# Both halves of a fold and all five chunks of a gather issued together, in a fused attention and feed-forward kernel

## The chip, the cores and the metric

The kernel runs on one core of a Trainium2 chip. The metric is device time in microseconds (us) of one execution. TensorE is called PE here (its matmuls; PEld is its weight loads), VectorE DVE, ScalarE ACT, GpSimd POOL and SyncE SP, as in the profile. Batches are counted from 0, so that the third batch is batch 2.

## The reference

Attention against 32 memory slots for each of 8 batches and 8 heads, then a feed-forward layer with the gate h cos(h) over all 4608 tokens:

```python
# q, k, v: (8, 8, 576, 64); phi: (8, 8, 576, 32); all float32
a = softmax(phi, axis=memory)                 # weights of each token over the 32 slots
k_m = einsum('bhsm,bhsd->bhmd', a, k)
v_m = einsum('bhsm,bhsd->bhmd', a, v)
attn = softmax(q @ k_m.T / 8) @ v_m           # (8, 8, 576, 64)
x = attn.transpose(0, 2, 1, 3).reshape(4608, 512)
h = x @ w_in                                  # w_in: 512 x 2048
out = (h * cos(h)) @ w_out                    # w_out: 2048 x 512
```

## The kernel before

**The main stream.** The 4608 tokens are worked in 12 groups of 384. For every group there are 16 steps f, one for each 128 of the 2048 hidden columns; a step has a number i = 16 * group + f. In a step `gemm1` (line 539) multiplies the softmax weights `aT` by a folded weight `vw` into the PSUM tile `hp` (6 matmuls of 384 columns, or 12 of 192 where a group spans two batches), `act` and `act_end` (lines 563 and 578) turn `hp` into `gp` on ACT and DVE by turns, and `gemm2` (line 591), four steps behind, multiplies `gp` by `w_out` into three accumulators `acc` (9 matmuls of 512 columns). `hp` has three PSUM buffers (line 80).

**The fold.** Since x = weights * v_m, the product v_m * w_in is formed once for each batch and called `vw`. It is made in four quarters q of 512 hidden columns, each in two halves g (`fold`, line 499). A half is `fold_psum` (line 472): for batches 2 to 7 eight matmuls with weights of 128 rows by 32 columns, four that run side by side in the four column strips of the array with the high part `vp` of the weights, and then four with the low part `vl`. The result is a PSUM tile `pv`, which `split_half` (line 487) reads twice: ACT writes its high part (line 490), then DVE its rest (line 492).

**The preparation of a batch.** `prep(b)` (line 525) is a generator that is advanced in the loop a few pieces at each step. Its first part `memory(b)` (line 273) makes the softmax of `phi`, then gathers k and v into the slots: five chunks of up to 128 tokens, each eight matmuls of 32 weight columns by 129 columns in float32 (line 241; the trace records each of them twice), all into one PSUM tile `psA`. After the last chunk it starts the loads of the next batch's `phi`, k and v, then divides by the sum (`X`, lines 307 to 313), transposes (`tpx`, line 317) and writes k_m and v_m out. Its second part `attend(b)` (line 440) has the scores `sc` (line 386, weights of 64 columns, in three blocks), softmax on DVE and ACT, and the transposes back into `aT`.

**What sets the order.** The tiles `psA`, `tpx`, `sc` and `pv` share one PSUM pool of two buffers, `ps_s` (lines 81 and 83): a third one waits until the first has been read. The first two batches are issued in an order written out by hand (line 50). From there on the loop (line 989) issues the steps; `folds` (line 985) says at which step a half is folded, `jobs` (line 982) between which steps a batch is prepared, and `NSTEP` (line 976) into how many pieces the preparation is counted for spreading it evenly over these steps. A scheduler then moves the issued instructions on each engine by their dependences.

Of the kernel before, what the change touches and what calls it, by code (L numbers as in the profile page):

```python
# [72 lines left out]
def attention_then_ffn(ctx: ExitStack, tc: tile.TileContext, phi, phiT, kv, kv_first, qT, w_in, w_out, eye, out):  # L73
# [9 lines left out]
    def small_ps(name):  # L83
        return ps_s.tile([P, 512], F32, tag="ps_s", name=name)
# [25 lines left out]
    def load_phi(b):  # L110
        if b < NT:
            loads["phiT", b] = t = ld.tile([P, 2, S], F32, tag="phiT", name=f"phiT_{b}", bufs=1)
            nc.sync.dma_start(out=t, in_=phiT[b, :, 0:S].rearrange("(g p) s -> p g s", p=P))
        a = ld.tile([P, 5, HM], F32, tag="phi", name=f"phi_{b}")
        nc.sync.dma_start(out=a[:, 0:4], in_=phi[b, 0:512].rearrange("(c p) m -> p c m", p=P))
        nc.sync.dma_start(out=a[0:S - 512, 4], in_=phi[b, 512:S])
        loads["phi", b] = a

    def load_kv(b):
        ts = []  # L120
        for c, (s0, n) in enumerate(TCH):
            t = ld.tile([P, H * KV], F32, tag="kv", name=f"kv_{b}_{c}", bufs=5)
            nc.sync.dma_start(out=t[:n], in_=kv[b, s0:s0 + n])
            ts.append(t)
        loads["kv", b] = ts
# [110 lines left out]
    def gather(psA, a, kvs, c, wide):  # L236
        n = TCH[c][1]
        for g in range(2):
            for j in range(4):
                h = 4 * g + j  # L240
                nc.tensor.matmul(psA[32 * j:32 * (j + 1), g * KV:g * KV + wide],  # L241
                                 lhsT=a[:n, c, h * M:(h + 1) * M], rhs=kvs[c][:n, h * wide:(h + 1) * wide],
                                 start=(c == 0 and g == 0), stop=(c == 4), skip_group_check=True)

    def blank(b):
        st["km", b] = wk.tile([P, NP, 2 * M], F32, tag="km", name=f"km_{b}", bufs=1)
        st["vm", b] = wk.tile([P, NP, 2 * M], F32, tag="vm", name=f"vm_{b}")
        nc.gpsimd.memset(st["km", b], 0.0)
        nc.gpsimd.memset(st["vm", b], 0.0)

    def spread_k(b, tpx):
        tv = tpx[:, 0:HM].rearrange("p (c t m) -> p c t m", t=2, m=M)
        nc.scalar.mul(st["km", b][0:D, :, 0:M], tv[0:D, :, 0], 1.0 / math.sqrt(D))
        nc.scalar.mul(st["km", b][D:P, :, M:2 * M], tv[D:P, :, 1], 1.0 / math.sqrt(D))
# [4 lines left out]
    def spread_v(b, tpx, copy):  # L259
        tv = tpx[:, 0:HM].rearrange("p (c t m) -> p c t m", t=2, m=M)  # L260
        copy(out=st["vm", b][D:P, :, 0:M], in_=tv[D:P, :, 0])
        copy(out=st["vm", b][0:D, :, M:2 * M], in_=tv[0:D, :, 1])

    def bound(b, X):
        l1 = wk.tile([P, 4], F32, tag="l1", name=f"l1_{b}")
        nc.vector.tensor_reduce(out=l1, in_=X.rearrange("p g (t d) -> p (g t) d", t=2), op=ALU.add, axis=AX.X,
                                apply_absolute_value=True)
        nc.vector.tensor_tensor(out=l1, in0=l1, in1=vmask.rearrange("p g t -> p (g t)"), op=ALU.mult)
        l2 = wk.tile([P, 1], F32, tag="l2", name=f"l2_{b}")
        nc.vector.tensor_reduce(out=l2, in_=l1, op=ALU.max, axis=AX.X)  # L270
        return l2

    def memory(b):
        a = loads.pop(("phi", b))
        if b < NT:

            nmx = wk.tile([P, 2], F32, tag="nmx", name=f"nmx_{b}", bufs=1)
            nc.vector.tensor_reduce(out=nmx, in_=loads.pop(("phiT", b)), op=ALU.max, axis=AX.X)
            top = small_ps(f"top_{b}")[:, 0:HM]
            for g in range(2):  # L280
                nc.tensor.transpose(top[:, g * P:(g + 1) * P], nmx[:, g:g + 1].broadcast_to([P, P]), ident)
        else:
            top = st["top", b]
        yield
        if b >= NT:
            yield
            yield
        for c0, c1, n in ((0, 4, P), (4, 5, S - 512)):
            ins = nc.vector.tensor_tensor(out=a[:n, c0:c1], in0=a[:n, c0:c1],
                                          in1=top[:n].unsqueeze(1).broadcast_to([n, c1 - c0, HM]),  # L290
                                          op=ALU.subtract)
            if b >= NT:

                tc.keep_in_program_order(ins)
            nc.scalar.activation(a[:n, c0:c1], a[:n, c0:c1], AF.Exp)
        yield
        yield
        kvs = loads.pop(("kv", b))
        psA = small_ps(f"psA_{b}")
        for c in range(5):  # L300
            gather(psA, a, kvs, c, KV)
            yield
        if b + 1 < B:
            load_phi(b + 1)
            load_kv(b + 1)
        pv = psA[:, 0:2 * KV].rearrange("p (g x) -> p g x", g=2)
        den = wk.tile([P, 2], F32, tag="den", name=f"den_{b}")
        nc.vector.tensor_scalar(out=den, in0=pv[:, :, 2 * D], scalar1=1e-9, scalar2=None, op0=ALU.add)
        nc.vector.reciprocal(out=den, in_=den)
        X = wk.tile([P, 2, P], F32, tag="X", name=f"X_{b}", bufs=1)  # L310
        for g in range(2):
            nc.vector.tensor_scalar(out=X[:, g], in0=pv[:, g, 0:2 * D], scalar1=den[:, g:g + 1], scalar2=None,
                                    op0=ALU.mult)
        yield
        tpx = small_ps(f"tpx_{b}")
        for g in range(2):
            nc.tensor.transpose(tpx[:, g * P:(g + 1) * P], X[:, g], ident)
        blank(b)
        spread_k(b, tpx)
        spread_v(b, tpx, nc.vector.tensor_copy)  # L320
        yield
        l2 = bound(b, X)
        l3 = wk.tile([P, 1], F32, tag="l3", name=f"l3_{b}")
        nc.gpsimd.partition_all_reduce(l3, l2, channels=P, reduce_op=RED.max)  # L324
        st["l3", b] = l3
        v_scale(b)
        yield


    def v_scale(b):  # L330
        ev = wk.tile([P, 1], F32, tag="ev", name=f"ev_{b}", bufs=2)
        power_of_two(ev, st["l3", b])
        st["ev", b] = ev
# [191 lines left out]
    def prep(b):  # L525
        yield from memory(b)
        yield from attend(b)
# [445 lines left out]
            yield  # L973

    REST = (18, 19, 20, 22, 24, 25)
    NSTEP = 24
    jobs, folds = [], {}
    for b in range(1, B):
        use = 48 * (b // 2) + 16 * (b % 2)
        before, length = {1: (3, 0), 2: (5, 13), 3: (6, 16)}.get(b, (6, 17) if b % 2 else (13, 18))  # L980
        if b > 1:
            jobs.append((b, use - before - length, use - before - 1))
        for q in range(NQ):
            for g in range(2):
                folds.setdefault(use - before + 4 * q + 2 * g, []).append((b, q, g))
    gens = {}
    rest = attend_rest()
    pending, begun = [(0, f, st["gp", f]) for f in range(NF - LAG, NF)], []
    for i in range(NF, 12 * NF):
# [29 lines left out]
        for b, s, e in jobs:  # L1019
# [3 lines left out]
            if s <= i <= e:  # L1023
                if b not in gens:
                    gens[b] = [prep(b), 0]
                want = math.ceil((i - s + 1) * NSTEP / (e - s + 1))
                while gens[b][0] is not None and gens[b][1] < want:
# [54 lines left out]
```

## Time and profile before

| what | value |
|---|---|
| median of 3 runs | 700.62 us (700.43 to 701.5) |
| the profiled execution's own time | 700.91 us |
| its span, first to last instruction | 699.1 us |
| PE busy | 691.4 us |
| DVE busy | 525.9 us |
| ACT busy | 503.1 us |
| POOL busy | 36.9 us |
| granted TensorE clock | 1.000 |

The profile is of one execution. The 1.8 us between its span and its own time lie before the first and after the last instruction. A row of the timeline gives the start of a group of like instructions, its length, the engine, the line, output<-inputs, the shape and how many; in brackets stands idle time before it and what ended that. PE overlaps one matmul with the next, so the time that a matmul takes from the others is the distance of two starts and not its own length.

### The profile page before, as it was taken

What the parts mean: (1) busy time and instruction counts of PE and PEld (TensorE: products, weight loads), DVE (VectorE), ACT (ScalarE), POOL (GpSimd) and SP (SyncE); (2) the same over time, 40 slices, a digit from 0 to 9 for tenths busy, and PEclk for the clock granted to TensorE, in tenths of its full rate; (3) what the DMA queues carried; (4) which work ended last, traced back from release to release, by engine and by line L of the source; (5) the groups of instructions that cost most, each with busy time, mean ns of one, the idle gap of its engine ahead of it and who ended that gap; (6) DMA issues with size and microseconds to landing.
All of it is one profiled execution on the core that took longest, in us unless ns stands there. A gap on an engine that the chain in (4) does not pass through costs nothing.

```text
span 699.1 us, 11806 instructions
## 1 busy us (share of the span) xinstructions
PE 691.4 (99%) x4588; PEld 354.8 (51%) x4588; DVE 525.9 (75%) x1118; ACT 503.1 (72%) x942; POOL 36.9 (5%) x50
## 2 busy tenths in 40 slices
PE   8999999999999999999999999999999999999997
PEld 4444445464544445555445445655445444565553
DVE  4887899999979875689657886589766986566552
ACT  3686888996976966868775876769767776665652
POOL 2423100000001000010000000000000000000000
PEclk9999999999999999999999999999999999999999
DMA  9999827109243100321105300142100100100101
GB/s 291 389 317 362 321 68 201 31 11 282 84 133 103 50 1 13 135 76 63 46 1 171 114 0 1 50 169 68 46 0 2 46 0 1 46 1 1 46 1 45
DMA packets 31480, 66.17 MB, mean 95 GB/s; under 512 B 2176, under 2 KB 11456, under 8 KB 31424
## 3 DMA queue, kind: packets, MB, share of 16 engines
q1 hardware_dynamic: 27104, 57.55, 25.5%
q10 hardware_dynamic: 4320, 7.87, 3.0%
q8 instruction: 36, 0.59, 0.4%
q14 instruction: 20, 0.16, 0.1%
HBM read 51.77 MB, written 9.44 MB: 88 GB/s over the span
## 4 chain that ended last, share of the span: by engine, by line
PE 81%; DVE 10%; ACT 4%; DMA 3%; issue 1%; SPq 0%; POOL 0%; DVEq 0%; ACTq 0%
PE acc L604 40%; PE hp L553 21%; PE acc L599 6%; PE pv L483 4%; PE hp L544 3%; PE psA L241 2%; DVE u L574 2%; PE sc L386 2%; DVE gp L586 1%; DMA phi<-in_phi 1%; DMA kv<-in_kv_first 1%; DVE u L583 1%; PE pvf L509 1%; PE pv L477 1%; ACT u L579 1%; ACT gp L585 1%
## 5 line engine op out<-in xcount | busy, mean ns | idle before, releaser
L604 PE MATMUL acc<-wo,gp 128*128 128x512 f16 x1584 | 372.2, 379 | 0.0
L604 PEld LDWEIGHTS <-gp 128*128 128x128 f16 x1584 | 153.4, 98 | 160.4 <-issue 2.1
L553 PE MATMUL hp<-aT,vw 128*128 128x192 f16 (+1 forms) x1440 | 203.5, 284 | 0.9 <-DVE u L583 0.8
L553 PEld LDWEIGHTS <-vw 128*128 128x128 f16 x1440 | 124.9, 98 | 82.1 <-issue 27.7
L579 ACT ACTIVATE u<-u,quarter 128x384 f32<-128x384 f32 x176 | 106.9, 614 | 68.8 <-DVE u L574 68.3
L583 DVE SCALAR_TENSOR_TENSOR u<-hp,u 128x384 f32<-128x384 f32 x176 | 96.5, 553 | 61.5 <-ACT u L579 60.9
L574 DVE SCALAR_TENSOR_TENSOR u<-hp,cu,gp 128x192 f32<-128x192 f32 (+1 forms) x240 | 115.3, 502 | 24.5 <-ACT gp L569 23.0
L569 ACT ACTIVATE gp<-hp,cu 128x192 int32<-128x192 f32 (+1 forms) x240 | 111.5, 491 | 22.5 <-PE hp L553 15.6
L586 DVE TENSOR_TENSOR gp<-u,gp 128x384 f16<-128x384 f32 x176 | 96.2, 551 | 34.5 <-ACT gp L585 33.9
L585 ACT CAST gp<-u 128x384 f16<-128x384 f32 x176 | 88.4, 509 | 43.9 <-DVE u L583 43.4
L599 PE MATMUL acc<-wo,gp 128*128 128x512 f32 x96 | 44.4, 596 | 0.0
L492 DVE SCALAR_TENSOR_TENSOR vw<-pv,vw 128x512 f16<-128x512 f32 x48 | 33.0, 688 | 7.0 <-ACT vw L490 6.5
L490 ACT ACTIVATE vw<-pv 128x512 f16<-128x512 f32 x48 | 28.4, 591 | 8.0 <-PE pv L483 7.5
L620 ACT ACTIVATE ob<-acc,os 128x512 f32<-128x512 f32 x28 | 18.5, 684 | 14.5 <-PE acc L604 11.9
L599 PEld LDWEIGHTS acc<-wo,gp 128*128 128x128 f32 x96 | 17.6, 191 | 17.9 <-issue 16.0
L544 PE MATMUL hp<-aT,vf 128*128 128x384 f32 x64 | 24.0, 499 | 0.0
L241 PE MATMUL psA<-kv,phi 128*32 128x129 f32 (+3 forms) x640 | 23.6, 276 | 0.2
L579 ACT ACT_TABLE_LOAD x18 | 23.1, 1283 | 0.3
L241 PEld LDWEIGHTS psA<-kv,phi 128*32 128x32 f32 (+1 forms) x640 | 16.1, 109 | 12.0 <-issue 6.9
L386 PE MATMUL sc<-q,km 128*64 128x256 f32 (+3 forms) x192 | 20.0, 336 | 0.1
L324 POOL PARTITION_ALL_REDUCE l<-l x6 | 3.0, 508 | 301.3 <-DVE l L270 301.3
L399 ACT ACT_TABLE_LOAD x14 | 18.0, 1283 | 0.3
(159 smaller groups left out, 544.6 us busy)
## 6 DMA issues: line engine op xcount, KB each, us to landing
kv<-in_kv SPq DMA_DIRECT2D x28, 516.0 KB, 5.5
raw_out<-in_w_out SPq DMA_DIRECT2D x8, 1024.0 KB, 8.1
q<-in_qT SPq DMA_DIRECT2D x7, 1152.0 KB, 5.6
out<-ob ACTq DMA_DIRECT2D x30, 256.0 KB, 2.2
raw_in<-in_w_in SPq DMA_DIRECT2D x6, 1024.0 KB, 12.3
phi<-in_phi SPq DMA_DIRECT2D x7, 512.0 KB, 5.2
w_in_sb<-w_in_parts SPq DMA_DIRECT2D x12, 256.0 KB, 5.6
phiT<-in_phiT SPq DMA_DIRECT2D x4, 576.0 KB, 6.9
```

The costliest lines, as they stand in the source:

```text
L241: nc.tensor.matmul(psA[32 * j:32 * (j + 1), g * KV:g * KV + wide], lhsT=a[:n, c, h * M:(h + 1) * M], rhs=kvs[c][:n, h * wide:(h + 1) * wid ...
L386: nc.tensor.matmul(sc[D * p:D * (p + 1), g * n:(g + 1) * n], lhsT=km[:, 2 * g + p], rhs=qt[:, 2 * g + p, t0:t0 + n], start=True, stop=True)
L544: nc.tensor.matmul(hp[:, :GT], lhsT=st["vf", q][:, g, fo * P:(fo + 1) * P], rhs=st["aTf"][:, g], start=(g == 0), stop=(g == 1))
L553: nc.tensor.matmul(hp[:, c0:c0 + n], lhsT=vw[:, wi, g, fo * P:(fo + 1) * P], rhs=aT[:, ai, g, c1:c1 + n], start=(k == 0), stop=(k == 5))
L569: ins = nc.scalar.activation(ni[:, c0:c0 + n], hp[:, c0:c0 + n], AF.Copy, scale=turns, bias=0.25)
L574: nc.vector.scalar_tensor_tensor(out=u[:, c0:c0 + n], in0=hp[:, c0:c0 + n], scalar=turns, in1=ni[:, c0:c0 + n], op0=ALU.mult, op1=ALU.subt ...
L579: nc.scalar.activation(u, u, AF.Sin, scale=TWO_PI_BELOW, bias=quarter)
L583: nc.vector.scalar_tensor_tensor(out=u, in0=hp[:, :GT], scalar=2.0 ** -17, in1=u, op0=ALU.mult, op1=ALU.mult)
L585: nc.scalar.copy(gp[:, 0], u)
L586: nc.vector.tensor_tensor(out=gp[:, 1], in0=u, in1=gp[:, 0], op=ALU.subtract)
L599: nc.tensor.matmul(accs[grp][t], lhsT=gp[:, t * P:(t + 1) * P], rhs=wo[:, f + 1], start=(f == 0), stop=(f == NF - 1))
L604: nc.tensor.matmul(accs[grp][t], lhsT=gp[:, gi, t * P:(t + 1) * P], rhs=parts[:, wi], start=(f == 0 and gi == 0 and wi == 0), stop=(f == N ...
```

## The change

```diff
         psA = small_ps(f"psA_{b}")
         for c in range(5):
             gather(psA, a, kvs, c, KV)
-            yield
+        yield
         if b + 1 < B:
             load_phi(b + 1)
             load_kv(b + 1)
...
-    NSTEP = 24
+    NSTEP = 20
...
-                folds.setdefault(use - before + 4 * q + 2 * g, []).append((b, q, g))
+                folds.setdefault(use - before + 4 * q + (2 * g if b < 2 else 0), []).append((b, q, g))
```

The five chunks of a gather, until now five pieces of the preparation, become one piece; since the generator has four pieces fewer, `NSTEP` goes from 24 to 20. For batches 2 to 7 the second half of a quarter is folded in the same step as the first, where it came two steps later. No instruction of the computation is added or left out; ACT gets two more loads of an activation table (the order has 19 at line 579 and 15 at line 399, from 18 and 14).

The first place is PE at the gather of batch 2. `psA` is the gathered tile, `kv_0` to `kv_4` are the chunks; the number at the end of a name only tells instances apart.

```order
 L241 MATMUL psA_1472<-kv_0_724,phi_721 32x129 x8
 L241 MATMUL psA_1472<-kv_1_726,phi_721 32x129 x8
 L241 MATMUL psA_1472<-kv_2_728,phi_721 32x129 x8
+L241 MATMUL psA_1472<-kv_3_730,phi_721 32x129 x8
+L241 MATMUL psA_1472<-kv_4_732,phi_721 32x129 x8
 L553 LDWEIGHTS vw_0_774
```

The last two chunks stood one step later, between `gemm2` and the next `gemm1`:

```order
 L604 MATMUL acc_2_1005<-wo,gp_13_1371 128x512
-L241 MATMUL psA_1472<-kv_3_730,phi_721 32x129 x8
-L241 MATMUL psA_1472<-kv_4_732,phi_721 32x129 x8
 L553 LDWEIGHTS vw_0_774
-L553 MATMUL hp_2_1570<-aT_678,vw_0_774 128x384
```

They moved up to the other three, so that the gather of this batch is one run of matmuls instead of two.

The second place is PE at quarter 2 of the fold of batch 4 (`pv_2_0` and `pv_2_1` are its halves), before:

```order
L483 LDWEIGHTS vl
L483 MATMUL pv_2_0_3816<-w_in_sb,vl 32x512
L553 LDWEIGHTS vw_3_3020
L553 MATMUL hp_12_3831<-aT_2229,vw_3_3020 128x384
L553 LDWEIGHTS vw_3_3020
```

and now:

```order
L483 LDWEIGHTS vl
L483 MATMUL pv_2_0_3816<-w_in_sb,vl 32x512
L483 LDWEIGHTS vp_3567
L483 MATMUL pv_2_1_3827<-w_in_sb,vp_3567 32x512
L483 LDWEIGHTS vp_3567
L483 MATMUL pv_2_1_3827<-w_in_sb,vp_3567 32x512
```

Where `gemm1` followed the first half, the second half follows it directly; two steps further on nothing stands in its old place.

The third place is DVE at quarter 1 of the fold of batch 2, while batch 3 is prepared (`vw_1<-pv_1_0` reads the first half, `at<-sc_0` the scores), before:

```order
L492 SCALAR_TENSOR_TENSOR vw_1_2118<-pv_1_0_2119,vw_1_2118 128x512
L586 TENSOR_TENSOR gp_15_2102<-u_15_2101,gp_15_2102 128x384
L574 SCALAR_TENSOR_TENSOR u_0_2156<-hp_0_2149,cu_1938,gp_0_2157 128x384
L229 TENSOR_TENSOR mx_2320<-phi_2130 128x512
L230 TENSOR_TENSOR mx_2320<-mx_2320 128x256
L583 SCALAR_TENSOR_TENSOR u_0_2156<-hp_0_2149,u_0_2156 128x384
L261 COPY vm_2177<-tpx_2173 64x4x32
```

and now:

```order
L492 SCALAR_TENSOR_TENSOR vw_1_2158<-pv_1_0_2159,vw_1_2158 128x512
L586 TENSOR_TENSOR gp_15_2142<-u_15_2141,gp_15_2142 128x384
L492 SCALAR_TENSOR_TENSOR vw_1_2158<-pv_1_1_2170,vw_1_2158 128x512
L574 SCALAR_TENSOR_TENSOR u_0_2198<-hp_0_2191,cu_1938,gp_0_2199 128x384
L392 STREAM_TRANSPOSE at_2182<-sc_0_2185 128x512
```

The two reads of the halves come with one instruction between them instead of eleven, and the read of the scores follows them closely.

Counted over the whole PE order from the gather of batch 2 on, a run being tiled matmuls (weights of 32 or 64 columns) with no matmul of 128 weight columns between them:

| runs that hold | before | now |
|---|---|---|
| gather of batch 2 | 2 | 1 |
| folds of batch 2, gather of batch 3 | 11 | 7 |
| folds of batch 3, gather of batch 4 | 10 | 5 |
| folds of batch 4, gather of batch 5 | 10 | 5 |
| folds of batch 5, gather of batch 6 | 10 | 6 |
| folds of batch 6, gather of batch 7 | 10 | 5 |
| folds of batch 7 | 8 | 4 |
| together | 61 | 33 |
| scores alone | 14 | 15 |

Of the 24 quarters 20 are now one run. The other four (quarters 0 of batches 2 and 5, quarters 3 of batches 3 and 5) are split by steps of the main stream. One run before held a half of a fold and a block of scores together; those scores now stand alone.

## The prediction

> **What bounds the kernel now.** I read the page first (busy times and durations), then the busy time by stretch, then the timeline of PE around single folds, gathers and scores, and last the rows in which PE stands idle. The page:
>
> ```profile
> span 699.1 us, 11806 instructions
> PE 691.4 (99%) x4588; PEld 354.8 (51%) x4588; DVE 525.9 (75%) x1118; ACT 503.1 (72%) x942; POOL 36.9 (5%) x50
> ...
> L604 PE MATMUL acc<-wo,gp 128*128 128x512 f16 x1584 | 372.2, 379 | 0.0
> ...
> L492 DVE SCALAR_TENSOR_TENSOR vw<-pv,vw 128x512 f16<-128x512 f32 x48 | 33.0, 688 | 7.0 <-ACT vw L490 6.5
> L490 ACT ACTIVATE vw<-pv 128x512 f16<-128x512 f32 x48 | 28.4, 591 | 8.0 <-PE pv L483 7.5
> ...
> L579 ACT ACT_TABLE_LOAD x18 | 23.1, 1283 | 0.3
> ```
>
> PE is busy for 99% of the span. The next view says whether that holds in the stretches that the change touches: 289 to 323 prepares a batch, 323 to 366 mostly folds.
>
> ```profile
> core 0: us, PE busy (x) PEld busy (x) DVE busy (x) ACT busy (x) POOL busy (x), PEclk, DMA share, GB/s
> ...
> 289.00:323.00 34.00, 33.60 (x309) 20.02 (x307) 28.48 (x74) 27.14 (x54) 2.15 (x4) 1.00 0.39 124
> 323.00:366.00 43.00, 43.00 (x258) 20.01 (x255) 28.93 (x56) 30.96 (x57) 0.00 (x0) 1.00 0.05 19
> ```
>
> PE has no idle time where a batch is folded and 0.4 us of 34 in the preparation, while DVE and ACT are at 67 to 84%. The clock is full. So time can come only out of PE's own work, or go into new waits of PE. The change adds and removes no matmul; what it can save lies between them. One half of a fold, alone between `gemm2` and `gemm1`:
>
> ```profile
> 208.91 1.03 PE L604 MATMUL acc<-wo,gp 128*128 128x512 f16 x4
> ...
> 209.87 0.10 PEld L483 LDWEIGHTS <-vp 128*32 128x32 f16 x4 [0.42 <-issue]
> 209.87 0.40 PE L483 MATMUL pv<-w_in_sb,vp 128*32 128x512 f16 x4
> 209.88 0.10 PEld L483 LDWEIGHTS <-vl 128*32 128x32 f16 x4
> 210.10 0.39 PE L483 MATMUL pv<-w_in_sb,vl 128*32 128x512 f16 x4
> ...
> 210.42 1.15 PE L553 MATMUL hp<-aT,vw 128*128 128x384 f16 x6
> ...
> 210.54 0.60 ACT L490 ACTIVATE vw<-pv 128x512 f16<-128x512 f32 x1 [0.53 <-PE pv L483]
> ...
> 211.40 1.24 PE L604 MATMUL acc<-wo,gp 128*128 128x512 f16 x5
> ...
> 211.61 0.69 DVE L492 SCALAR_TENSOR_TENSOR vw<-pv,vw 128x512 f16<-128x512 f32 x1
> ```
>
> A group's last matmul starts one matmul length before the group's end. The four `acc` matmuls take 1.03 us and one takes 0.379, so they start (1.03 - 0.38) / 3 = 0.22 apart, and the last starts at 208.91 + 1.03 - 0.38 = 209.56. After it the tiled matmuls should start at 209.78; they start at 209.87, 0.09 late. Their two waves of four are 0.23 apart, about the 0.22 of any 512 columns. The next full matmul should start 0.22 after the second wave and starts 0.32 after. From `acc` to `hp` it is 210.42 - 209.56 = 0.86; less the 0.22 that `acc` takes anyway, the half costs 0.64 us, of which two waves are 0.43 or 0.44. **About 0.2 us goes at the two ends of the run**, where PE changes between full and tiled matmuls and shows as busy.
>
> **The price of a change, from runs that are already joined.** One chunk of a gather alone, and a half joined with one chunk:
>
> ```profile
> 364.98 0.59 PE L604 MATMUL acc<-wo,gp 128*128 128x512 f16 x2
> 365.51 0.65 PE L241 MATMUL psA<-kv,phi 128*32 128x129 f32 x16
> 366.09 0.82 PE L604 MATMUL acc<-wo,gp 128*128 128x512 f16 x3
> ```
> ```profile
> 201.16 0.59 PE L604 MATMUL acc<-wo,gp 128*128 128x512 f16 x2
> 201.69 0.40 PE L483 MATMUL pv<-w_in,vp 128*32 128x512 f16 x4
> 201.91 0.39 PE L483 MATMUL pv<-w_in,vl 128*32 128x512 f16 x4
> 202.13 0.61 PE L241 MATMUL psA<-kv,phi 128*32 128x129 f32 x16
> 202.67 1.15 PE L553 MATMUL hp<-aT,vw 128*128 128x384 f16 x6
> ```
>
> In the same way the chunk costs 366.09 - (364.98 + 0.59 - 0.38) - 0.22 = 0.68, and half and chunk together 202.67 - (201.16 + 0.59 - 0.38) - 0.22 = 1.08. Apart they would be 0.64 + 0.68 = 1.32, so the joint saves 0.24. A half joined with a block of scores, whose weights have 64 columns, and such a block alone:
>
> ```profile
> 216.05 0.59 PE L604 MATMUL acc<-wo,gp 128*128 128x512 f16 x2
> 216.58 0.40 PE L483 MATMUL pv<-w_in_sb,vp 128*32 128x512 f16 x4
> ...
> 217.12 1.08 PE L386 MATMUL sc<-q,km 128*64 128x256 f32 x8
> 218.14 1.15 PE L553 MATMUL hp<-aT,vw 128*128 128x384 f16 x6
> ```
> ```profile
> 307.33 0.81 PE L604 MATMUL acc<-wo,gp 128*128 128x512 f16 x3
> 308.07 1.08 PE L386 MATMUL sc<-q,km 128*64 128x256 f32 x8
> 309.09 1.08 PE L553 MATMUL hp<-aT,vw 128*128 128x192 f16 x11
> ```
>
> Together 218.14 - 216.26 - 0.22 = 1.66, the scores alone 309.09 - (307.33 + 0.81 - 0.38) - 0.22 = 1.11: this joint saves only 0.64 + 1.11 - 1.66 = 0.09, since the tile shape still changes inside it.
>
> **The change part by part.**
>
> *The runs.* By the count above the PE order has 61 - 33 = 28 fewer runs of folds and gathers. Twenty are quarters whose halves now touch. No run of before has two halves in a row, so this price is estimated: by its two waves a half costs 0.43 within a run against 0.64 alone, which saves 0.21; the ends are 0.09 (different tile shapes) and 0.24 (half and chunk, same shape). I take 0.21, since the two halves have one shape. 20 x 0.21 = 4.2 us. The other eight are joints with or inside gathers, at 0.24: 1.9 us. The scores that no longer touch a half give back 0.09. On PE together 4.2 + 1.9 - 0.1 = **6.0 us**, all of it where PE sets the pace.
>
> *The second half comes two steps earlier.* ACT and DVE then get the reads of both halves in one step: 2 x 0.59 and 2 x 0.69 us, where they had one each. With the pair such a step lasts longer on PE, by 0.64 + 0.43 us, so about half of these reads is paid by the step itself; the rest delays `gp`, which `gemm2` needs four steps later. At 67 and 72% busy in the folding stretch that is caught up; I take nothing. If that cover is gone, the price is that of the second rival below.
>
> *Two buffers of `ps_s`.* A pair holds both, so whatever needs one next waits for the DVE read of the first half. That read ended at 211.61 + 0.69 = 212.30, 2.43 us after the half had begun. Nearly everywhere the next user comes one preparation piece or four steps later. At quarter 1 of batch 2 and quarter 3 of batch 6 it is a block of scores after only one `gemm1`: counted from the pair's start, the fourth wave starts after 0.23 + 2 x 0.22 = 0.67, the first `hp` matmul 0.32 later, and the scores after six of these (211.40 - 210.42 = 0.98) and the 0.09 of a run's beginning: 2.06 us in all. The scores come 2.43 - 2.06 = 0.4 us too early. Price between nothing (DVE free at once) and 0.4 each; I take 0.2 + 0.2 = 0.4 us.
>
> *Waits that stood before.* PE's idle rows from batch 2 on that are longer than 0.25 us:
>
> ```profile
> 186.58 0.59 PE L604 MATMUL acc<-wo,gp 128*128 128x512 f16 x2
> 187.53 0.65 PE L553 MATMUL hp<-aT,vw 128*128 128x384 f16 x3 [0.36 <-DVE u L583]
> ```
> ```profile
> 196.35 0.40 PE L483 MATMUL pv<-w_in,vl 128*32 128x512 f16 x4 [0.33 <-DVE vl L355]
> ```
> ```profile
> 248.92 0.40 PE L483 MATMUL pv<-w_in,vp 128*32 128x512 f16 x4 [0.39 <-ACT vp L354]
> ```
> ```profile
> 321.88 0.48 PE L553 MATMUL hp<-aT,vw 128*128 128x384 f16 x2 [0.40 <-DVE u L583]
> ```
>
> Together 1.5 us. Two of them are `hp` waiting in the softmax of a prepared batch, two are the first fold of a batch waiting for its weights. With the pieces spread differently each may grow or go; I keep the sum, and put 1 us on either side into the range.
>
> *Steps and loads.* Gather, `X` and `tpx` come earlier in a preparation, and with them the loads of the next batch, which are far from late (SP only issues them; PE's idle rows name no DMA). All five chunks must have landed at the first one's place; they were loaded a batch ahead. The two more table loads cost ACT 2 x 1.28 us, beside PE's work while ACT is at 80% in a preparation.
>
> **Sum.** 6.0 - 0.4 = 5.6 us. The profiled execution took 700.91, so 695.3; the median of the runs shown is 0.3 lower, so the forecast is **695.0 us**. About 0.2% (1.4 us) is what a measurement of this kernel can tell from no change.
>
> **The rivals.**
>
> *The joint of two halves is worth less (chance 0.13).* The weights of the second half's first wave could come only when the first half's second wave runs; PEld's 0.10 us would then stand between the waves. For it: no such joint is in the trace. Against it: the `vl` loads start at 209.88, 0.01 after the first wave, and the second wave comes at the pace of the columns. Price 20 x 0.10 = 2.0, time 697.0. The Trainium skill, "TensorE: Matmul & The Clock Gate", part 3 on packing small matmuls, says that weight loads overlap matmuls in flight only when their row groups differ; here all tiles use all 128 rows, so by that rule each wave would follow its loads. The rows above do not agree with it: the `vl` loads (209.88 and 0.10 long) lie under the first wave.
>
> *Evacuation becomes the bound (chance 0.05, slower).* Both reads of a pair push `act_end` back in the queues of ACT and DVE, `hp` of three steps ago is not read in time, and PE stands as it did at 187.53 and 321.88. There PE stood idle for 0.36 and 0.40 us; counted from start to start, `hp` was due 0.22 after the last `acc` (186.58 + 0.59 - 0.38 + 0.22 = 187.01) and came at 187.53, 0.5 us late. At 0.5 in every one of 24 quarters that is 12 us against 6.0: 700.6 + 6.0 = 706.6. It turns the sign from 0.25 us per quarter on. For it: DVE and ACT at 80% and more in the preparations. Against it: both waits stood in a softmax with its table loads, none at a fold. The Trainium skill, "TensorEngine Tiling (Array Packing)", on the PSUM bottleneck, says that tiling speeds up TensorE but not the emptying of PSUM, which may then become the bottleneck; at single halves no row here shows it.
>
> *New waits for the two buffers (chance 0.11).* Not two places but some eight (the split quarters, and `tpx` and scores near a pair) lose 0.4 us each: 3.2 in place of 0.4, 697.8.
>
> *It does nothing (chance 0.03).* The 0.2 us at the ends would be needed by PE anyway, for instance in filling and emptying, and reappear inside the pairs: 700.6. The joint of half and chunk speaks against it. That the scheduler undoes the change is excluded by its order, in which 20 of 24 quarters touch.
>
> **How the numbers follow.** The forecast has the remaining 0.68. Its own range: all 28 joints at 0.24 and 1 us of the old waits gone is 700.6 - 6.7 - 1.0 = 692.9; the joints at their price with 1 us of new waits beside the 0.4 is 696.0. The first and third rivals are taken in up to 697.8, which leaves out less than 2 in 10: 692.9 to 697.9. Faster by over 0.2%: 0.68 + 0.13 + 0.11 = 0.92; within: 0.03; slower: 0.05.
>
> **What would show it.** Right: a pair as four waves 0.22 to 0.23 apart and 1.29 us from `acc` to `hp`; PE's busy time down by about 6; a gather of five chunks as one run; DVE and ACT busy as before (ACT plus 2.6). The two early blocks of scores with a short wait for DVE L492. Wrong: a gap of 0.1 or more between the second and third wave; idle rows of PE at `hp`, naming DVE L583, right after pairs; a sum of PE's idle rows that grows by more than 2 us.

## The result and the profile after

| | before | changed |
|---|---|---|
| median of 6 runs, us | 700.76 (700.43 to 701.5) | 697.12 (696.37 to 697.36) |
| ratio to before, 95% interval | 1 | 0.9945 [0.9932, 0.9958] |
| the profiled execution, us | 700.91 | 696.7 |
| its span, us | 699.1 | 694.9 |

The changed kernel is 3.6 us faster by the medians, 3.9 us by the ratio and 4.2 us by the two profiled executions. The forecast was 5.6 us and 695.0 us, so the measured 697.12 us lies 2.1 us above it and inside its range of 692.9 to 697.9 us.

The page of the changed kernel, busy times and the two groups that read a fold out of PSUM:

```profile
span 694.9 us, 11834 instructions
PE 685.2 (99%) x4588; PEld 358.8 (52%) x4588; DVE 525.1 (76%) x1118; ACT 502.9 (72%) x944; POOL 35.7 (5%) x50
...
L492 DVE SCALAR_TENSOR_TENSOR vw<-pv,vw 128x512 f16<-128x512 f32 x48 | 32.0, 685 | 2.2 <-ACT vw L490 2.1
L490 ACT ACTIVATE vw<-pv 128x512 f16<-128x512 f32 x48 | 27.0, 589 | 5.0 <-PE pv L483 5.0
```

PE has the same 4588 matmuls and is busy 6.2 us less. The busy times by stretch, the first the preparation of batch 4, the second mostly folds:

```profile
core 0: us, PE busy (x) PEld busy (x) DVE busy (x) ACT busy (x) POOL busy (x), PEclk, DMA share, GB/s
288.00:322.00 34.00, 33.41 (x312) 20.43 (x310) 30.50 (x80) 28.53 (x57) 2.05 (x4) 1.00 0.39 124
322.00:364.00 42.00, 42.00 (x249) 20.17 (x248) 27.81 (x52) 28.57 (x54) 0.00 (x0) 1.00 0.05 20
```

PE is still full in the folds and idle for 0.6 us in the preparation, where it was 0.4. One pair of halves, alone between `gemm2` and `gemm1`:

```profile
344.96 0.59 PE L604 MATMUL acc<-wo,gp 128*128 128x512 f16 x2
345.49 0.10 PEld L483 LDWEIGHTS <-vp 128*32 128x32 f16 x4 [0.42 <-issue]
345.49 0.40 PE L483 MATMUL pv<-w_in_sb,vp 128*32 128x512 f16 x4
345.50 0.11 PEld L483 LDWEIGHTS <-vl 128*32 128x32 f16 x4
345.71 0.39 PE L483 MATMUL pv<-w_in_sb,vl 128*32 128x512 f16 x4
345.72 0.11 PEld L483 LDWEIGHTS <-vp 128*32 128x32 f16 x4
345.93 0.39 PE L483 MATMUL pv<-w_in_sb,vp 128*32 128x512 f16 x4
...
346.15 0.39 PE L483 MATMUL pv<-w_in_sb,vl 128*32 128x512 f16 x4
...
346.47 1.15 PE L553 MATMUL hp<-aT,vw 128*128 128x384 f16 x6
346.58 1.08 ACT L490 ACTIVATE vw<-pv 128x512 f16<-128x512 f32 x2
```

Four waves, 0.22 apart. From the last `acc` (344.96 + 0.59 - 0.38 = 345.17) to `hp` it is 1.30 us, less 0.22 for `acc` 1.08, where two lone halves cost 1.28. The weights of each wave load under the wave before it, those of the second half too (345.72, with the wave of 345.71 in flight).

What did not go as forecast stands at batch 3, around the pair of quarter 1 of batch 2:

```profile
206.49 0.27 ACT L253 ACTIVATE km<-tpx 64x128 f32<-64x128 f32 x1 [0.34 <-PE tpx L317]
...
208.42 0.69 DVE L229 TENSOR_TENSOR mx<-phi 128x512 f32<-128x512 f32 x1 [1.65 <-DMA phi<-in_phi]
209.15 0.29 DVE L261 COPY vm<-tpx 64x128 f32<-64x128 f32 x1
209.24 0.40 PE L483 MATMUL pv<-w_in_sb,vp 128*32 128x512 f16 x4
...
209.47 0.39 PE L483 MATMUL pv<-w_in_sb,vl 128*32 128x512 f16 x4
210.03 0.28 DVE L262 COPY vm<-tpx 64x128 f32<-64x128 f32 x1
...
210.46 0.40 PE L483 MATMUL pv<-w_in_sb,vp 128*32 128x512 f16 x4 [0.60 <-DVE vm L262]
...
210.87 0.61 ACT L579 ACTIVATE u<-u,quarter 128x384 f32<-128x384 f32 x1 [2.69 <-DVE u L574]
...
211.39 0.58 ACT L490 ACTIVATE vw<-pv 128x512 f16<-128x512 f32 x1
...
212.24 0.67 DVE L492 SCALAR_TENSOR_TENSOR vw<-pv,vw 128x512 f16<-128x512 f32 x1
...
213.01 1.08 PE L386 MATMUL sc<-q,km 128*64 128x256 f32 x8 [0.85 <-POOL mx L232]
```

DVE stands 1.65 us at line 229, the first max over the next batch's `phi`, until its load lands. Behind it in DVE's queue are the copies of v_m out of `tpx` (lines 261 and 262). The second half of the fold needs the buffer of `tpx` and comes at 210.46, 0.99 after the wave before it where 0.22 to 0.23 is usual: 0.75 us lost. ACT stands 2.69 us for DVE, so the first half is read late. Its DVE read ends at 212.91, and the scores that need its buffer start at 213.01, 0.92 us after their turn. (The row names POOL, whose instruction also ended then; an experiment below speaks for the buffer.)

### The profile page after: what moved, and what is told of

Read it like the earlier page. It is cut to its first block, busy times and chain, and to the rows that moved or that the text cites. A ratio compares the mean times of both kernels' runs of the same rounds, so it can differ in the third digit from the quotient of the medians.

```text
span 694.9 us, 11834 instructions
## 1 busy us (share of the span) xinstructions
PE 685.2 (99%) x4588; PEld 358.8 (52%) x4588; DVE 525.1 (76%) x1118; ACT 502.9 (72%) x944; POOL 35.7 (5%) x50
## 4 chain that ended last, share of the span: by engine, by line
PE 80%; ACT 7%; DVE 7%; DMA 3%; SPq 1%; issue 1%; POOL 0%; DVEq 0%; ACTq 0%
PE acc L604 41%; PE hp L553 22%; PE acc L599 6%; PE hp L544 3%; PE pv L483 3%; DMA raw_in<-in_w_in 2%; PE sc L386 2%; ACT u L579 1%; DVE gp L586 1%; PE pvf L509 1%; ACT gp L569 1%; PE pv L477 1%; PE psA L241 1%; DMA kv<-in_kv 1%; ACT L579 1%; ACT gp L585 1%
## 5 line engine op out<-in xcount | busy, mean ns | idle before, releaser
L553 PEld LDWEIGHTS <-vw 128*128 128x128 f16 x1440 | 127.0, 98 | 80.2 <-issue 18.6
L490 ACT ACTIVATE vw<-pv 128x512 f16<-128x512 f32 x48 | 27.0, 589 | 5.0 <-PE pv L483 5.0
L579 ACT ACT_TABLE_LOAD x19 | 24.4, 1283 | 0.3
L241 PE MATMUL psA<-kv,phi 128*32 128x129 f32 (+3 forms) x640 | 21.3, 276 | 0.0
L399 ACT ACT_TABLE_LOAD x15 | 19.2, 1283 | 0.3
L386 PEld LDWEIGHTS sc<-q,km 128*64 128x64 f32 x192 | 11.4, 136 | 12.4 <-issue 6.2
```

The source lines that it names most:

```text
L386: nc.tensor.matmul(sc[D * p:D * (p + 1), g * n:(g + 1) * n], lhsT=km[:, 2 * g + p], rhs=qt[:, 2 * g + p, t0:t0 + n], start=True, stop=True)
L553: nc.tensor.matmul(hp[:, c0:c0 + n], lhsT=vw[:, wi, g, fo * P:(fo + 1) * P], rhs=aT[:, ai, g, c1:c1 + n], start=(k == 0), stop=(k == 5))
L579: nc.scalar.activation(u, u, AF.Sin, scale=TWO_PI_BELOW, bias=quarter)
```

## The experiments

Every kernel was timed against the kernel before on its own chip; the runs of before had a median of 701.21 us for the first four and 700.45 us for the last four, so ratios compare better than medians. "Runs" are runs of folds and gathers from batch 2 on, counted in the trace. "Rest" is from the first matmul of group 1 (line 553, at 94.8 to 96.5 us) to the end, which leaves out the first loads of the kernel, whose length differs between executions by up to 1.7 us. "Waits" is PE's lost time in it: where the distance between two starts of matmuls is over 0.06 us longer than it usually is for these two kinds, the excess counts.

| kernel | median, us | ratio [95%] | runs | rest, us | waits, us | rest less waits |
|---|---|---|---|---|---|---|
| before | 700.76 | 1 | 61 | 603.6 | 2.8 | 600.8 |
| changed | 697.12 | 0.9945 [0.9932, 0.9958] | 33 | 599.5 | 4.6 | 594.9 |
| folds only | 699.86 | 0.9990 [0.9976, 1.0005] | 43 | 602.9 | 5.9 | 597.1 |
| gather only | 699.44 | 0.9983 [0.9974, 0.9992] | 52 | 602.1 | 3.1 | 598.9 |
| same step, apart | 699.35 | 0.9974 [0.9963, 0.9985] | 53 | 602.1 | 2.9 | 599.2 |
| changed, max pinned | 695.48 | 0.9916 [0.9902, 0.9930] | 33 | 598.1 | 3.1 | 594.9 |
| before, max pinned | 699.84 | 0.9989 [0.9980, 0.9997] | 61 | 602.8 | 1.9 | 600.9 |
| folds only, max pinned | 696.79 | 0.9941 [0.9928, 0.9954] | 43 | 599.4 | 2.3 | 597.1 |
| gather only, max pinned | 698.60 | 0.9978 [0.9967, 0.9988] | 52 | 601.5 | 2.6 | 598.9 |
| pinned, scales early, quarter 3 late | 696.10 | 0.9932 [0.9920, 0.9943] | 32 | 598.5 | 3.8 | 594.7 |

**Folds only.** Of the change, the line of `folds` alone:

```diff
-                folds.setdefault(use - before + 4 * q + 2 * g, []).append((b, q, g))
+                folds.setdefault(use - before + 4 * q + (2 * g if b < 2 else 0), []).append((b, q, g))
```

> Only the two halves of a quarter are issued together; the gather stays in five pieces and NSTEP at 24. Its PE order has 43 runs of folds and gathers against 61 before and 33 after, and 15 runs of scores alone. Theory (a run of tiled matmuls costs 0.21 us at its two ends): 18 x 0.21 = 3.8 us less, 0.1 back for the scores, and no new wait for the phi load, since the gather ends where it did before: 696.5 to 697.5. Rival (the gain comes from the pieces of the preparation moving earlier): no more than 1 us less, 700.

Measured 0.9990, an interval that holds no change: the time of the rival, but not for its reason. PE's work fell by 600.8 - 597.1 = 3.7 us, as the theory has it, and its waits grew by 3.1. The largest, at the first scores of batch 4:

```profile
301.24 0.69 DVE L229 TENSOR_TENSOR mx<-phi 128x512 f32<-128x512 f32 x1 [2.94 <-DMA phi<-in_phi]
...
302.32 0.74 DVE L574 SCALAR_TENSOR_TENSOR u<-hp,cu,gp 128x192 f32<-128x192 f32 x2
...
303.09 0.62 ACT L579 ACTIVATE u<-u,quarter 128x384 f32<-128x384 f32 x1 [2.98 <-DVE u L574]
...
303.73 0.27 ACT L254 ACTIVATE km<-tpx 64x128 f32<-64x128 f32 x1
...
304.11 1.08 PE L386 MATMUL sc<-q,km 128*64 128x256 f32 x8 [1.43 <-issue]
```

DVE waits 2.94 us for the load, ACT behind it for DVE, k_m behind that in ACT's queue, and the scores for k_m: 1.50 us of PE. The row itself says "issue", so that the scores waited for k_m is read from the order of the rows; a pinned run below tests it. The theory had said that this wait would not be there, and was wrong in that.

**Gather only.** The other two edits:

```diff
             gather(psA, a, kvs, c, KV)
-            yield
+        yield
...
-    NSTEP = 24
+    NSTEP = 20
```

> Only the gather is in one piece and NSTEP 20; the second half of a quarter stays two steps later. 52 runs of folds and gathers, 11 of scores alone. Theory: 9 x 0.23 = 2.1 us less and 0.3 from three runs of scores that touch a half, 698.4; with the wait for the phi load at batch 3, which would then come from the earlier pieces, up to 1.7 back, 700.1. Rival (the waits come from the paired halves alone): 698.4 with no wait for the phi load.

Measured 0.9983, 1.2 us by the ratio, about half of the theory's 2.4; the trace gives 1.5. PE's work fell by 1.9 us; new waits for X and for the emptying of accumulators, less the waits that went, took 0.3 back. DVE stood 1.3 us at line 229 and no row of PE hangs on it. So the rival was right that this part alone brings no wait of PE for the load, but its time of 698.4 was not reached.

**Same step, apart.** The changed kernel with the halves of a quarter in one step, but the first ahead of `gemm1`:

```diff
+        for b, q, g in folds.get(i, ()):
+            if b >= 2 and g == 0:
+                if q == 0:
+                    scales(b)
+                fold(b, q, g)
         hp = gemm1(grp, f)
...
         for b, q, g in folds.get(i, ()):
+            if b >= 2 and g == 0:
+                continue
             if q == g == 0:
                 scales(b)
             fold(b, q, g)
```

> The changed kernel, but the first half of a quarter is issued ahead of the step's gemm1 and the second behind its gemm2: both in one step as in the changed kernel, but 15 or more full matmuls between them on PE. 53 runs of folds and gathers, 14 of scores alone. Theory: the joints of halves are gone, so 20 x 0.21 = 4.2 us come back: 701 if all waits of the changed kernel stay, 699 if those at batch 3 go. Rival (the gain comes from having both halves in one step): as the changed kernel, 697.

Quarter 0 of batch 4 in it: the first half ahead of `hp`, then the 15 full matmuls of the step, then the second half:

```profile
329.07 0.40 PE L483 MATMUL pv<-w_in,vp 128*32 128x512 f16 x4
329.30 0.39 PE L483 MATMUL pv<-w_in,vl 128*32 128x512 f16 x4
329.62 1.15 PE L553 MATMUL hp<-aT,vw 128*128 128x384 f16 x6
330.60 2.10 PE L604 MATMUL acc<-wo,gp 128*128 128x512 f16 x9
332.64 0.40 PE L483 MATMUL pv<-w_in,vp 128*32 128x512 f16 x4
332.87 0.39 PE L483 MATMUL pv<-w_in,vl 128*32 128x512 f16 x4
333.19 1.15 PE L553 MATMUL hp<-aT,vw 128*128 128x384 f16 x6
```

Measured 699.35 us, near the 699 that the theory gives when the waits at batch 3 go, as they did in its trace, and not the rival's 697. Its 20 more runs cost 599.2 - 594.9 = 4.3 us of PE, 0.22 each. What is saved is the joint on PE, not that both halves belong to one step.

**Changed, max pinned.** Line 229 keeps its issued place on DVE:

```diff
-        nc.vector.tensor_tensor(out=mx[:, 0:2], in0=a[:, 0:2], in1=a[:, 2:4], op=ALU.max)
+        tc.keep_in_program_order(nc.vector.tensor_tensor(out=mx[:, 0:2], in0=a[:, 0:2], in1=a[:, 2:4], op=ALU.max))
```

> The changed kernel, with the first max over the next batch's phi (line 229) kept in the issued order on DVE, where the scheduler had moved it ahead of the copies of v_m while its load was still under way. Theory: DVE then doesn't stand for 1.65 us at batch 3, and PE's two waits there (0.75 us in the fold, 0.92 at the scores) go but for 0.0 to 0.4 us for the two PSUM buffers: 1.3 to 1.7 us less than the changed kernel, 695.4 to 695.8. Rival (the two PSUM buffers alone make these waits): no change, 697.1.

The same place as above in this kernel:

```profile
208.20 0.29 DVE L261 COPY vm<-tpx 64x128 f32<-64x128 f32 x1
...
208.51 0.28 DVE L262 COPY vm<-tpx 64x128 f32<-64x128 f32 x1
...
210.36 0.40 PE L483 MATMUL pv<-w_in_sb,vp 128*32 128x512 f16 x4
210.59 0.39 PE L483 MATMUL pv<-w_in_sb,vl 128*32 128x512 f16 x4
...
210.81 0.39 PE L483 MATMUL pv<-w_in_sb,vp 128*32 128x512 f16 x4
...
212.28 1.29 DVE L492 SCALAR_TENSOR_TENSOR vw<-pv,vw 128x512 f16<-128x512 f32 x2
212.33 0.38 PE L604 MATMUL acc<-wo,gp 128*128 128x512 f16 x1
213.07 1.08 PE L386 MATMUL sc<-q,km 128*64 128x256 f32 x8 [0.36 <-issue]
```

DVE waits for no load, the halves touch, and PE's 0.75 us are gone. The pin also takes the max's own 0.69 us of work away from this place, but the wait alone is enough to explain the loss: without its 1.65 us the second copy would have ended at 210.31 - 1.65 = 208.66 in the changed kernel, before the second half's turn at 209.69. At the scores 0.43 us stay: two reads of a pair take 1.29, so the first ends at about 212.97, and the scores follow 0.1 later, as they did in the changed kernel. That is the price of the two PSUM buffers; the other half of the 0.92 was the load. The median is 695.48, at the lower end of what the theory gave. That is 1.6 us below the changed kernel's; the ratios differ by 2.0 us and their intervals do not touch; in the traces the rest is 1.4 us shorter. It is the fastest kernel of the study.

**Before, max pinned.** The same edit in the kernel before.

> The kernel before with line 229 kept in the issued order on DVE, nothing else. In its trace DVE stood 2.7 us at line 229 for the phi load, in three places, but no idle row of PE names what came of it. Theory (the phi load costs only where PE's next work hangs on what DVE has queued behind): no change, 700.2 to 701.2. Rival (the pin is a gain of its own that has nothing to do with the change): 1.4 us less or more, 699.3.

Measured 0.9989, 0.8 us faster, between the two and nearer to the theory's side, but not nothing: the theory was wrong that the load cost PE nothing before. The rows of the kernel before and of this one on DVE and PE:

```profile
299.60 0.69 DVE L229 TENSOR_TENSOR mx<-phi 128x512 f32<-128x512 f32 x1 [1.41 <-DMA phi<-in_phi]
...
L553 PE MATMUL hp<-aT,vw 128*128 128x384 f16 (+1 forms) x1080 | 158.6, 289 | 0.8 <-DVE u L583 0.8
```
```profile
L553 PE MATMUL hp<-aT,vw 128*128 128x384 f16 (+1 forms) x1084 | 159.3, 289 | 0.4 <-DVE u L583 0.4
```

Of the two waits of `hp` in the kernel before, the one at 321.88, twenty-two us behind the load, is gone with the pin, and with it three shorter ones; 0.9 us in all. That DVE carried the delay this far is likely but not tested: between the end of the max at 300.29 and 321.88 it was busy for 20.31 of 21.59 us in the kernel before, so it had little idle time in which to catch up.

**Folds only and gather only, max pinned.** The first two experiments with the same edit.

> The first experiment (halves issued together, gather in five pieces) with line 229 kept in the issued order. There DVE stood 5.4 us for the phi load and PE lost 1.50 and 0.68 us at the first scores of batches 4 and 6. Theory: these two waits go, 2.2 us less than the first experiment: 697.3 to 698.3. Rival (the scores wait for the PSUM buffers that a pair and a gather in pieces hold): no more than 0.5 us less, 699.4.

> The second experiment (gather in one piece, halves two steps apart) with line 229 kept in the issued order. DVE stood 1.3 us there and PE lost nothing by it that its rows tell. Theory: no change, 699.0 to 699.8. With the last two experiments and the pinned changed kernel it makes a table of four, in which the two parts should add up: the pinned changed kernel's gain less that of the pinned folds is that of the pinned gather, within 0.7 us. Rival (the two parts need one another): the sum of the two is over 1 us short of both together.

Folds only fell from 0.9990 to 0.9941 and its waits from 5.9 to 2.3 us; the two at the scores are gone, so they were the load's and not the buffers'. The gather alone went from 0.9983 to 0.9978, within their intervals no change. In the pinned kernels the parts add up: rest falls by 602.8 - 599.4 = 3.4 us for the folds, by 1.3 for the gather, by 4.7 for both. Unpinned they are 0.7, 1.5 and 4.1: the two parts seemed to need one another, and what they needed was only that the load be waited for at another place. This rests on the traces. By the ratios the pinned folds and gather give 3.4 and 0.8 us over the pinned kernel before, and both together 5.1. That leaves 1.0 us open where 0.7 was expected, but with intervals of 0.6 to 1.0 us to either side of each ratio the times can't tell.

**Pinned, scales early, quarter 3 late.** Two attempts at the waits that were left:

```diff
+        for b, q, g in folds.get(i + 2, ()):
+            if q == g == 0 and b >= 2:
+                scales(b)
         for b, q, g in folds.get(i, ()):
-            if q == g == 0:
+            if q == g == 0 and b < 2:
                 scales(b)
...
-                folds.setdefault(use - before + 4 * q + (2 * g if b < 2 else 0), []).append((b, q, g))
+                folds.setdefault(use - before + 4 * q + (2 * g if b < 2 else 2 * (q == 3 and b in (3, 5))), []).append((b, q, g))
```

> The pinned changed kernel, with the scales of a batch (line 335, the weights vp and vl of its first fold) issued two steps ahead of that fold, and quarter 3 of batches 3 and 5 folded two steps later, behind the gather's X, so that its halves touch. Theory: of the waits left, 0.44 and 0.07 us at the first fold of batch 2 and 0.35 twice at the second half of quarter 3 go, and one run: 1.0 to 1.4 us less than the pinned changed kernel, 694.1 to 694.6. Rival (the waits only move to the next user of the two PSUM buffers): no change, 695.5.

There was no gain: 696.10, above the 694.1 to 694.6 of the theory and near the rival's 695.5. PE's three kinds of wait in it:

```profile
195.35 0.40 PE L483 MATMUL pv<-w_in,vp 128*32 128x512 f16 x4 [0.70 <-DVE phi L289]
```
```profile
213.32 0.83 PE L386 MATMUL sc<-q,km 128*64 128x256 f32 x5 [0.99 <-issue]
```
```profile
294.05 0.30 PE L317 MATMUL tpx<-ident,X 128*128 128x128 f32 x1 [0.41 <-DVE X L312]
```

One run fewer, but the second half at batch 2 now waits longer for line 289 on DVE, which reads a tile of the same two buffers (0.78 us for 0.44); the row of the changed kernel at 193.94 names the same line, so that wait was not one for the scales. The scores wait longer for the pair (1.06 for 0.43), and where quarter 3 had waited, `tpx` does (0.57 for 0.35, twice). The first two are waits for the two buffers, as the rival has it; the third names `X`, which `tpx` reads.

## Why the prediction was right, and where it was off

**The price of a run: right.** A pair was forecast at 1.29 us from `acc` to `hp` and measured 1.30, its waves 0.22 to 0.23 apart. The last column of the table follows the number of runs: 28 fewer give 5.9 us, 18 give 3.7, 9 give 1.9, 20 more give 4.3 back, that is 0.21 to 0.22 each. The forecast for all runs was 6.0 us, and PE's busy time fell by 6.2.

**The rival of the weight loads: refuted.** No wave of a pair waits for its weights, and the time that this rival gave, 697.0, is near the measured one by coincidence. In its list of what overlaps, the Trainium skill ("TensorE: Matmul & The Clock Gate", part 3 on packing small matmuls) has weight loads overlap only with matmuls of other row groups; the rows at 345.50 and 345.72 do not agree with that, since all tiles there use the same 128 rows.

**The rival of evacuation: refuted as a cause of loss at the pairs.** Where batches are folded PE is full, 42.00 of 42.00 us, and none of the waits lies behind a pair but the scores at batch 3 and the split quarters.

**Two buffers: one place right, one nothing, three missed.** I put 0.4 us at most on the scores at quarter 1 of batch 2 and at quarter 3 of batch 6, and took half. Without the load's wait the first is 0.43. The second is nothing: the scores start 0.03 late. The split quarter 3 of batches 3 and 5, which I named only in a rival, loses 0.35 each, and the second half of the first fold of batch 2 loses 0.44. Without the load's wait that is four places and 1.6 us where I had put 0.4; the third rival had some eight places and 3.2 us.

**The step that failed is "Steps and loads".** I wrote that the next batch's loads "are far from late" since PE's idle rows name no DMA. PE never waits for them, but DVE does, in program order with everything behind it, and PE waits for that. Of the 1.7 us that PE lost at batch 3, 0.43 stay without the load's wait and belong to the buffers; the other 1.2 are most of the 1.4 us by which the two traces (4.2, that is joints 5.9 less 1.8 more of waits, rounded) fall short of the forecast of 5.6. The row for it was in the trace of before, DVE's 2.7 us at line 229, and I had asked only for PE's idle rows. That these waits cost 0.9 us before already, by way of `hp`, I had kept as softmax work.

**Luck in the old waits.** I kept the sum of the waits that stood before, and outside batch 3 it did stay, 2.9 us against 2.8. But they are other waits. The 0.5 us at 187.53 and the two of 0.4 and 0.46 for a fold's weights are gone, and the 0.44 and twice 0.35 us named above are new. Nothing in the forecast says that these cancel.

**ACT.** The 2.6 us of two more table loads were forecast on ACT's busy time; it went from 503.1 to 502.9. The loads are there (24.4 for 23.1 at line 579, 19.2 for 18.0 at line 399). Against them stands that reads back to back overlap (two of 0.59 take 1.08 above, and line 490 is busy 27.0 for 28.4). The rest is overlap between different lines: each line for itself, ACT's busy times add up to 542.5 us before and 544.9 after, while the engine's total, which counts overlapping time once, does not grow.

## What to carry to other kernels

Where TensorE is full, count how often it changes between full and tiled matmuls: a run of tiled matmuls costs a fixed time at its ends, so group what has the same tile shape, and take the price from runs that are already grouped. When pieces are moved, look at the engines that wait without being the bottleneck: an instruction that waits for a load stops all that is queued behind it, here 1.65 us of DVE, and a scheduler may put it too early, here some 22 us ahead of its issued place (208.42 for 231.9 with the pin). Two edits that seem to help one another may only be shifting the same wait, so test each with that wait taken away.

## What the runs showed of the hardware

- Between full matmuls of 128 weight columns and tiled ones of 32, PE loses 0.09 us on the way in (209.87 for 209.78 in the kernel before) and 0.10 on the way out (0.32 from the last wave at 346.15 to `hp` at 346.47, for 0.22), without a row that shows it as idle.
- Column tiles load the next wave's weights under the wave in flight, over four waves at a pace of 0.22 us (345.49 to 346.15).
- An idle row understates what PE loses, since the matmul before it is drawn longer than its turn: 0.60 us idle at 210.46 were 0.75 us lost, 0.36 at 187.53 were 0.5.
